# Nine-row loads for two batches, joint attention tails, k split over two queues, and two x tiles by DMA transpose, in a fused linear-attention and Swish-MLP kernel

## Chip, cores, metric

One core of one Trainium2 chip. The metric is the device time of one execution in microseconds (us), the median of several executions; lower is better.

## The reference, cut to what matters

```python
def _attn_ref(q, k, v):                      # 8 batches, 8 heads, 576 rows, 64 columns, f32
    def phi(x): return np.where(x > 0, x, np.exp(x) - 1.0) + 1.0
    q_p, k_p = phi(q), phi(k)
    kv  = np.einsum('bhsd,bhse->bhde', k_p, v)
    z   = np.sum(k_p, axis=2)
    num = np.einsum('bhsd,bhde->bhse', q_p, kv)
    den = np.einsum('bhsd,bhd->bhs', q_p, z)[..., None] + 1e-06
    return num / den

def _moe_ref(x, w_in, w_out, beta):          # x is 4608 x 512, w_in 512 x 2048, w_out 2048 x 512
    h = x @ w_in
    g = h * (1.0 / (1.0 + np.exp(-beta * h)))
    return g @ w_out
```

The attention's output, heads side by side, is the x of the second part.

## The kernel before

Attention (kv, q transposes, num, normalisation, x transposes) is threaded through the large matmuls: H (x times w_in, then Silu) and Y (times w_out) of one batch after the other. The attention of batch b+1 is done during Y of batch b. TensorE does all the matmuls, so below "H1" means the stretch of H matmuls of batch 1, and "Y1" that of its Y matmuls.

576 rows are four tiles of 128 and a tail of 64. Two layouts are used. In the *row form* (all batches but 0) a tensor lies on 128 partitions, four rows of each of eight heads, and the tail on 64 partitions in a second copy. In the *nine-row form* (batch 0 only) half of the heads lie on partitions 0 to 63 and half on 64 to 127, nine consecutive rows on each partition.

```python
def load_rows(dst, src, b, eng=nc.gpsimd):            # row form
    eng.dma_start(out=dst[:, :, 0:NJ, :]...,          # 128 partitions, rows of 512 B
                  in_=src[b, :, 0:MAIN, :].rearrange("h (p j) d -> p h (j d)", j=NJ))
    eng.dma_start(out=dst[0:TAIL, :, NJ, :],          # 64 partitions, rows of 128 B
                  in_=src[b, :, MAIN:S, :].rearrange("h s d -> s h d"))

def load_nine(dst, src, h0=0, h1=HH, j0=0, j1=N9):    # nine-row form, batch 0
    for g in range(2):
        nc.gpsimd.dma_start(
            out=dst[g * TAIL : (g + 1) * TAIL, h0:h1, j0:j1, :]...,     # 64 partitions
            in_=src[0, g * HH + h0 : g * HH + h1, :, :]...)
# ... (cut)
load_nine(k9, k); load_nine(q9, q, j1=4)
# ... identity, v9 in two parts, the rest of q9
for i in range(4):
    nc.gpsimd.dma_start(out=w_in_sb[i], in_=w_in_v[:, :, i * 512 : (i + 1) * 512])
load_w_out(0); load_w_out(1)          # 2 x 512 KB each, f32, 128 partitions, scaled later
load_k(1); load_q(1)
# ... (cut) after the start of batch 0:
load_w_out(2); load_v(1); load_w_out(3)
```

TensorE's start, with warm-up matmuls before there is data, and Y of batch 0 with the attention of batch 1 in it:

```python
warm(10); beta_trans(); make_beta(); warm(20)
exp0(1, 0, 5); ...                               # phi of k, then of q, then kv, num, x of batch 0
# ... (cut)
relu(1, 1); relu(1, 0); w_out_scale(2); phi(1, 1)
v_copy(1)                                        # VectorE, needs v(1)
phi(1, 0)
y_phase_wide(0, {
    9:  [F(kv_mm, 1), F(kv_evac, 1), F(w_out_scale, 3)],
    10: [F(q_trans, 1, 0, 1, wide=True), F(q_trans, 1, 2, 3, wide=True)],
    11: [F(num_mm, 1, 0), F(num_norm, 1, 0)],
    12: [F(num_mm, 1, 1), F(num_norm, 1, 1), F(x_trans, 1, 0, wide=True)],
    # ... (cut)
})
```

Batches 0 to 2 transpose their x tiles on TensorE, batches 3 to 7 by DMA transposes on SyncE's queue (`by_dma(b)`: b >= 3). Each batch has its own tail step of four matmuls with 64 rows of output.

## Time and profile before

297.17 us median of three runs. Starts and lengths of the stretches, read from the timeline of TensorE (first H or Y matmul of each batch), in us:

| | H0 | Y0 | H1 | Y1 | H2 | Y2 | H3 |
|---|---|---|---|---|---|---|---|
| start | 17.16 | 34.16 | 52.53 | 67.61 | 85.25 | 101.19 | 116.38 |
| length | 17.00 | 18.37 | 15.08 | 17.64 | 15.94 | 15.19 | 14.67 |

The bare matmuls of an H or a Y take 13.8 us (64 of 0.216). What a stretch has above that is attention work or waiting; Y0, H0 and Y1 have the most. The lines for this are in the prediction below. The traces' short names: PE is TensorE and PEld its weight loads, DVE VectorE, ACT ScalarE, POOL GpSimd, SPq SyncE's queue. PSUM is the memory that TensorE writes its results to. A timeline line gives: start, duration, engine, line of the source, operation, output and inputs, shape, number of instructions, and in brackets the idle time before it and what ended that.

### The profile page before, as it was taken

To read this page: it belongs to the slowest core of one execution; us is meant where nothing else is said; L and a number is where in the kernel's file an instruction comes from. 1 tells how busy PE (TensorE), PEld (TensorE's weight loads), DVE (VectorE), ACT (ScalarE), POOL (GpSimd) and SP (SyncE) were. 2 spreads that over 40 slices of the span, in tenths; PEclk is the share of its full clock that TensorE was granted. 3 is DMA by queue.
4 is the path that set the end of the run, shared out by engine and by line. 5 is a ranking of instruction groups with operands and counts; after the bars stand their busy time and mean duration, and the time that the engine had idled before them with its cause. 6 is when DMAs were issued, how large, how long until landed. Compare 5 with 4: busy or idle time off the path is not lost.

```text
span 295.1 us, 4750 instructions
## 1 busy us (share of the span) xinstructions
PE 283.9 (96%) x1891; PEld 143.9 (49%) x1912; DVE 124.0 (42%) x261; ACT 175.1 (59%) x234; POOL 52.7 (18%) x72
## 2 busy tenths in 40 slices
PE   8879999999999999999999999999999999999994
PEld 3557445644465544445444544454445444444444
DVE  4765488504365174616461646154715400110012
ACT  2788786889988780778087907790770077018500
POOL 8924474540003200330023000000000000000000
PEclk9999999999999999999999999999999999999999
DMA  7999999999637993699369945024502400120032
GB/s 103 196 207 343 256 272 192 256 193 192 89 142 100 175 131 113 130 174 154 98 129 159 159 109 124 2 71 116 127 0 72 118 36 0 38 90 16 0 73 71
DMA packets 72310, 37.09 MB, mean 126 GB/s; under 512 B 40912, under 2 KB 66784, under 8 KB 72288
## 3 DMA queue, kind: packets, MB, share of 16 engines
q0 software_dynamic: 38912, 20.45, 47.9%
q1 hardware_dynamic: 33216, 16.20, 22.9%
q8 instruction: 15, 0.25, 0.3%
q10 hardware_dynamic: 160, 0.13, 0.2%
q14 instruction: 7, 0.06, 0.1%
HBM read 36.71 MB, written 9.44 MB: 156 GB/s over the span
## 4 chain that ended last, share of the span: by engine, by line
PE 76%; DMA 9%; POOL 4%; ACT 4%; issue 4%; DVE 1%; ACTq 0%; POOLq 0%; DVEq 0%
PE mm L453 37%; PE mm L505 33%; DMA xT<-in_moe_w_out_dram 5%; DMA vraw<-in_v_dram 4%; PE att L399 3%; ACT e L229 2%; POOL xqk L131 1%; PE att L344 1%; PE mm L537 1%; POOL w_in L159 1%; ACT L229 1%; POOL vraw L131 1%; ACT g L445 1%; DVE qk_p L242 0%; POOL xqk L111 0%
## 5 line engine op out<-in xcount | busy, mean ns | idle before, releaser
L445 ACT ACTIVATE g<-mm,beta_c 128x512 bf16<-128x512 f32 (+2 forms) x156 | 97.3, 633 | 88.4 <-PE mm L453 88.1
L505 PE MATMUL mm<-w_out,g 128*128 128x512 bf16 x541 | 126.7, 379 | 1.2 <-issue 0.3
L453 PE MATMUL mm<-xT,w_in 128*128 128x512 bf16 (+2 forms) x560 | 108.1, 349 | 1.4 <-DMA w_in<-in_moe_w_in_dram 1.1
L453 PEld LDWEIGHTS <-w_in 128*128 128x128 bf16 x656 | 61.9, 98 | 62.4 <-DMA w_in<-in_moe_w_in_dram 1.2
L505 PEld LDWEIGHTS <-g 128*128 128x128 bf16 x560 | 53.0, 98 | 58.2
L515 DVE COPY y_sb<-mm 128x512 f32<-128x512 f32 x27 | 18.7, 691 | 70.6 <-PE mm L505 69.1
L229 ACT ACTIVATE e<-xqk 128x2560 bf16<-128x2560 bf16 x14 | 31.9, 2329 | 0.1
L415 DVE TENSOR_TENSOR xs<-att,rden 128x512 bf16<-128x512 f32 (+1 forms) x40 | 27.6, 689 | 1.4
L242 DVE TENSOR_TENSOR qk_p<-r,e 128x2560 bf16<-128x2560 bf16 x14 | 20.9, 1490 | 13.1 <-ACT e L229 12.4
L355 DVE CAST kv_bd<-att 64x130 bf16<-64x130 f32 x28 | 8.2, 292 | 32.2 <-PE att L344 31.8
L72 POOL DMA_DIRECT2D vraw<-in_v_dram x7 | 6.4, 909 | 84.2 <-DVE vaug L370 78.5
L413 DVE TENSOR_SCALAR den<-att 128x8 f32<-128x8 f32 (+1 forms) x40 | 6.5, 161 | 32.0 <-PE att L399 31.9
L399 PE MATMUL att<-kv_bd,q_pT 128*128 128x130 bf16 (+1 forms) x160 | 15.8, 221 | 1.1 <-DVE kv_bd L370 0.7
L399 PEld LDWEIGHTS <-q_pT 128*128 128x128 bf16 (+1 forms) x160 | 11.6, 100 | 10.7 <-DVE xs L415 2.4
L453 PE MATMUL mm<-xT_tail,w_in 128*128 128x512 bf16 x63 | 13.9, 379 | 0.1
L237 DVE TENSOR_SCALAR r<-xqk 128x2560 bf16<-128x2560 bf16 x14 | 11.6, 834 | 3.8 <-DMA xqk<-in_q_dram 2.3
L575 PE MATMUL mm<-g 128*128 128x512 bf16 x34 | 9.9, 452 | 1.2 <-DVE g L143 1.2
L229 ACT ACT_TABLE_LOAD x7 | 9.0, 1283 | 0.1
L414 DVE RECIPROCAL rden<-den 128x8 f32<-128x8 f32 (+1 forms) x40 | 8.1, 202 | 1.4
L72 POOL DMA_DIRECT2D xqk<-in_k_dram x7 | 6.9, 984 | 6.3 <-DMA w_in<-in_moe_w_in_dram 2.8
L76 POOL DMA_DIRECT2D xqk<-in_k_dram x7 | 7.4, 1057 | 1.5 <-DMA w_in<-in_moe_w_in_dram 1.3
L256 ACT ACTIVATE e<-xqk 128x1280 bf16<-128x1280 bf16 (+1 forms) x4 | 4.4, 1155 | 5.4 <-DMA xqk<-in_k_dram 5.3
(71 smaller groups left out, 140.0 us busy)
## 6 DMA issues: line engine op xcount, KB each, us to landing
out_dram<-y_sb SPq DMA_DIRECT2D x28, 256.0 KB, 2.3
xqk<-in_k_dram POOLq DMA_DIRECT2D x7, 512.0 KB, 10.7
xqk<-in_q_dram POOLq DMA_DIRECT2D x7, 512.0 KB, 11.3
vraw<-in_v_dram POOLq DMA_DIRECT2D x7, 512.0 KB, 11.3
w_in<-in_moe_w_in_dram POOLq DMA_DIRECT2D x4, 512.0 KB, 11.0
g<-in_moe_w_out_dram POOLq DMA_DIRECT2D x4, 512.0 KB, 10.9
out_dram<-y_sb SPq DMA_DIRECT2D x14, 128.0 KB, 5.2
xqk<-in_moe_w_out_dram POOLq DMA_DIRECT2D x2, 512.0 KB, 14.4
```

Source lines behind the costliest of these rows:

```text
L72: eng.dma_start(out=dst[:, :, 0:NJ, :].rearrange("p h j d -> p h (j d)"), in_=src[b, :, 0:MAIN, :].rearrange("h (p j) d -> p h (j d)", j=NJ),)
L229: nc.scalar.activation(st[b, "e", a][:, h0:h1], xqk[b % NX][:, a, h0:h1], ACTF.Exp)
L237: nc.vector.tensor_scalar(st[b, "r", a][:, h0:h1], xqk[b % NX][:, a, h0:h1], 0.0, 1.0, ALU.max, ALU.add)
L242: nc.vector.tensor_tensor(st[b, "p"][:, a].rearrange("p j (h d) -> p h j d", h=H)[:, h0:h1], st[b, "r", a][:, h0:h1], st[b, "e", a][:, h0: ...
L355: nc.vector.tensor_copy(kv_bd[b % 2][i][gs, :, g, :], st[b, "kvp"][gs, 2 * i : 2 * i + 2, :])
L399: nc.tensor.matmul(nps[:n, p // 2, c0 : c0 + 2 * (D + 1)], st[b, "qT"][:, t, p, :n], kv_bd[b % 2][p // 2][:, p % 2], start=True, stop=True ...
L415: nc.vector.tensor_mul(xs[:n], nv[:, :, :, 0:D], rden[:n, :, :, None].to_broadcast([n, 2, 4, D]))
L445: nc.scalar.activation(g_sb[b % 2][:, ff, c0:c1], hp[:, c0:c1], ACTF.Silu, scale=beta_c[:, ff : ff + 1],)
L453: nc.tensor.matmul(hp[:, c0:c1], w_in_sb[ff // 4][:, kc, (ff % 4) * P : (ff % 4 + 1) * P], x[:, t0:t1, kc, :] if b < B else x[:, kc, c0:c1 ...
L505: nc.tensor.matmul(yp, g_sb[b % 2][:, ff, t * P : (t + 1) * P], w_out_sb[ff // 4][:, ff % 4, :], start=(ff == 0), stop=(ff == FC - 1),)
L515: nc.vector.tensor_copy(y_sb, yp)
L575: nc.tensor.matmul(st["warm"], g_sb[0][:, FC - 1, 0:P], g_sb[0][:, FC - 1, :], start=True, stop=True, skip_group_check=True,)
```

## The change

The intent is to shorten TensorE's work and waits outside the bare matmuls: load batch 1 in the nine-row form as well (fewer, longer rows; tails of two batches become one step), bring in k of batch 0 by two queues, and give batch 2's last two x tiles to the DMA. The core of the diff (helper functions, evictions and moved steps are cut):

```diff
-        load_nine(dst, src, h0=0, h1=HH, j0=0, j1=N9)        # batch 0 only
+        load_nine(dst, src, b, j0=0, j1=N9, eng=nc.gpsimd)   # any batch, any queue
...
+    load_nine(k_last, k, 0, KF, N9, eng=nc.sync)             # 4 of 9 rows of k, f32, SyncE's queue
-    nc.sync.dma_start(out=beta_row, ...)
+    nc.scalar.dma_start(out=beta_row, ...)
-    load_nine(k9, k)
+    load_nine(x9[0][1][:, :, 0:KF], k, 0, 0, KF)             # 5 of 9 rows, GpSimd
...
-    load_k(1)
-    load_q(1)
+    load_nine(x9[1][1], k, 1)
+    load_nine(x9[1][0], q, 1)
...
-    load_v(1)
+    load_nine(v9[1], v, 1)
...
-    make_beta()
-    warm(20)
+    warm(15)
...                                                          # num: tails of batches b-1 and b together
+            for i in range(1 if t < NJ else 2):
+                bb, n, r0 = (b, P, 0) if t < NJ else (b - 1 + i, TAIL, i * TAIL)
+                nc.tensor.matmul(nps[r0 : r0 + n, ...], st[bb, "qT"][:, t, p, :n], kv_bd[bb % 2]..., ...)
...
-        return b >= DMA_T
+        return b > 2 or (b == 2 and t >= 2) or t == NJ       # x by DMA transpose; all joint tails too
...                                                          # store of batch 1: two copies of 64 rows
-            if b == 0:
+            if b < 2:
...                                                          # batch 2
-                [(ff, 0, 2) for ff in range(4)] + [(ff, 2, 4) for ff in range(4)] + ALL[4:]
+                [(ff, 0, 2) for ff in range(8)] + [(ff, 2, 4) for ff in range(8)] + ALL[8:]
-            plan = { 0: [F(x_trans, 2, 2), F(num_mm, 2, 4), ...], 1: [F(x_trans, 2, 3)], 3: [F(x_trans, 2, 4)] }
...                                                          # later tails: every second batch
-            for t in range(NT):
+            for t in range(NT if n % 2 else NJ):
```

## The prediction

> **What bounds the kernel now.** I read the page first (engine shares, chain), then the busy table by stretches of 2 us for the start, then the timeline of the first 110 us, then the SyncE queue's own timeline, because that queue gets new work.
>
> ```profile
> PE 283.9 (96%) x1891; PEld 143.9 (49%) x1912; DVE 124.0 (42%) x261; ACT 175.1 (59%) x234; POOL 52.7 (18%) x72
> PE 76%; DMA 9%; POOL 4%; ACT 4%; issue 4%; DVE 1%; ACTq 0%; POOLq 0%; DVEq 0%
> ```
>
> TensorE sets the end: from about 85 us on it runs matmuls back to back, and one batch takes 29.85 us (first matmul on H of batch 3 at 116.38, of the later ones every 29.9). A matmul with 512 columns costs 0.216 us there (eight take 1.73 in the chain), so H and Y of a batch are 128 x 0.216 = 27.6 us and cannot move. Whatever the change gains lies in the other work on TensorE, in its waits before 88 us, and in the start.
>
> ```profile
> 2.00:4.00 2.00, 2.00 (x6) 0.73 (x5) 1.60 (x10) 0.23 (x2) 2.00 (x5) 1.00 0.70 97
> 4.00:6.00 2.00, 2.00 (x7) 0.56 (x6) 0.14 (x1) 0.00 (x0) 1.85 (x7) 1.00 1.15 185
> 6.00:8.00 2.00, 2.00 (x11) 0.94 (x10) 1.39 (x6) 0.51 (x1) 2.00 (x4) 1.00 1.24 154
> ...
> 14.00:16.00 2.00, 1.59 (x19) 0.70 (x16) 1.74 (x6) 1.98 (x2) 0.61 (x1) 1.00 1.23 208
> ```
>
> The last column is GB/s: 4 in the first 2 us, 97 in the next two, 154 to 185 to 8 us, then about 205 to 20 us. The transfers are full from 8 us on and short before. What it costs is in the timeline:
>
> ```profile
> 7.49 3.16 ACT L256 ACTIVATE e<-xqk 128x1280 bf16<-128x1280 bf16 x3 [5.25 <-DMA xqk<-in_k_dram]
> ...
> 17.16 1.07 PE L453 MATMUL mm<-xT,w_in 128*128 128x128 bf16 x16 [1.10 <-DMA w_in<-in_moe_w_in_dram]
> ...
> 41.91 1.27 DVE L370 COPY vaug<-vraw 128x2560 bf16<-128x2560 bf16 x1 [0.69 <-DMA vraw<-in_v_dram]
> ...
> 48.69 0.40 PE L433 MATMUL att<-identity,xs 128*128 128x128 bf16 x4
> ...
> 83.07 0.38 PE L433 MATMUL att<-identity,xs 128*128 128x128 bf16 x4 [0.61 <-ACT xT L372]
> ...
> 110.84 0.42 PE L399 MATMUL att<-kv_bd,q_pT 128*64 128x130 bf16 x4
> 111.19 4.86 PEld L505 LDWEIGHTS <-g 128*128 128x128 bf16 x24
> ```
>
> H of batch 0 starts at 17.16 because the first quarter of w_in lands then; attention had its x at 16.3. Batch 1's v lands at 41.9, and from there VectorE works without a pause (v copy, phi of q, four evictions, four w_out scalings, first normalisation) to 48.63; the first x transpose of batch 1 waits for that at 48.69. At 83.07 TensorE waits for an ACT eviction behind a table load.
>
> **What the Trainium skill says.** "DMA: Bandwidth & Descriptors", Issuing engines are not separate DMA queues: copies started from different engines run on the same 16 DMA engines, a second issuer saves only issue time. The trace agrees that the rate is common (205 GB/s of cast data from 8 us on), so the second queue can only fill the short stretch before 8 us. The same page, SWDGE vs HWDGE vs iDMA: a casting DMA must come from GpSimd; hence the SyncE part of k lands as f32 in an idle piece of g. "TensorEngine Tiling (Array Packing)", Key Properties: tiles work independently, but changing the mode drains the array. The trace shows both: 40 matmuls of 65 columns in 128*64 mode take 0.82 us with the pipe, 16 ns apart, less than the 27 ns of one 65-column stream (65/512 x 0.216); and four tail matmuls hold TensorE 0.35 us (110.84 to 111.19) where four 128*128 ones hold it 0.23 (102.92 to 103.15). "Perfetto Trace Analysis", DMA Instruction — HWDGE: a DMA's bar on its queue is descriptor work, not the moving of data. The trace agrees: a transpose of x has a bar of 1.19 us and lands 2.5 us after its start.
>
> **The change, part by part.**
>
> Start. k is split: five of nine rows by GpSimd with cast (two times 160 KB instead of 288), four by SyncE in f32. The bytes read are the same; the gain is what flows before GpSimd's descriptors are there. Up to 8 us the table lacks, against 0.2 MB per us, 0.2 MB in 2 to 4, 0.03 in 4 to 6, 0.09 in 6 to 8: 0.32 MB or 1.6 us. I take 1.25 of it. Then k is complete near 6.1 to 6.4 instead of 7.45, and w_in lands near 15.9. The three exps (3.16 us of ACT) and the kv and x chain move the same 1.2 us, so w_in stays the last thing to arrive. Five warm-up matmuls less (1.1 us) keep TensorE free for the earlier phi. The relu on f32 is slower; by the f32 scalings of w_out (0.48 us for 512 elements) 0.9 instead of about 0.58 us, beside ACT's exps. Gain at H0's start: 1.25 us.
>
> H0. Removed: four tail num matmuls (21.42 to 21.77, 0.35) and the tail transpose (23.96 to 24.18, 0.22). Gain 0.57, so Y0 could start near 32.3 instead of 34.16.
>
> Y0. It does not get all of that. Batch 1 comes in the nine-row form (GpSimd: two copies per tensor with 64x4 rows of 1152 B instead of 1024 rows of 512 B and 512 of 128 B), which I credit with 0.2 us per tensor: k, q and v of batch 1 took about 3.0, 3.3 and 3.3 us between landings, near the rate of the nine-row loads of batch 0. v(1) then lands at 41.9 - 1.25 - 0.6 = 40.05. VectorE from there: copy 0.75 to 1.2, phi 1.33 (1.47 x 2304/2560), clearing the tails 0.75 (new here), evictions 1.2, ones 0.2 (new here), scalings 1.68, normalisation 1.06: 7.0 to 7.45, against 6.75 before. First x transpose at 47.3 against 48.69: gain 1.4. TensorE's own work (kv as 36 matmuls of 130 columns in row pairs, 18 x 0.055 = 1.0 us instead of 0.66; q transposes 36 x 0.0145 = 0.52 instead of 0.97) would have been ready near 46.0, so VectorE after v is the bound. The rest of Y0 has its old 3.84 us. Sum at H1's start: 1.4.
>
> H1. No tail transpose (0.22); the joint tail is eight matmuls in two column halves, about what four cost. Sum 1.65.
>
> Y1. x(2,0) and x(2,1) leave by VectorE, and the second transpose sits one step later. From num(2,0) at 79.33 the steps are: y 0.86, num 0.22, wait for xs to 1.63, y 0.86, num, y 0.86, transpose, then num(2,3), which needs num(2,2)'s buffer and waits for VectorE to about 4.3, y 0.86: 5.42 us instead of 5.92 (79.33 to 85.25). The wait of 0.6 for ACT goes, one of 0.3 for VectorE comes. Gain 0.5, sum 2.15.
>
> H2. Removed: three transposes and the tail num, with their switches. H2 took 15.94 us (85.25 to 101.19) against 64 x 0.216 + 0.75 for kv = 14.57; I take 1.15 of the 1.37. Added: a wait. SyncE must first issue the stores of Y1, which are now two of 64 rows each:
>
> ```profile
> L492 SPq DMA_DIRECT2D out_dram<-y_sb x8: 466/563/603, 49.0 to 53.9; - x8
> ...
> 104.51 1.19 SPq L419 DMA_TRANSPOSE xT<-xs  x1
> ```
>
> In old times: the first y leaves ACT at 82.55 (table load), four stores of 0.47 to 0.56 end at 84.4 to 84.8, transpose(2,2) 1.2, two stores, transpose(2,3) starts at 86.6 to 87.2 and lands 2.5 later, at 89.1 to 89.7. H2 starts at 84.75 and eight half groups of 4 x 0.108 last 3.46, to 88.2. So TensorE waits 0.9 to 1.5 unless the queue is quicker than I count; I enter 0.9. Gain 0.25, sum 2.4.
>
> Later tails. Batches 4 and 6 lose their tail num (0.35 each); batches 3, 5 and 7 do two in about the time of one (plus 0.03 each). Gain 0.6, **sum 3.0 us**. The end, from Y of the tail rows, is not touched.
>
> **Rivals.** (a) The start gives nothing, because both queues share the engines and k's first part is held up by the f32 part. For it: the skill's rule. Against it: the measured hole of 97 GB/s. Then 1.25 is lost at H0 and at v(1): 295.4. (b) v(1) is not the bound: the nine-row loads are much quicker, and Y0 runs at TensorE's pace; 1.0 to 1.3 us more, 293.0. For it: the table's DMA share rises to 1.5 to 1.6 with the many-row loads, against about 1.25 with nine-row ones, at equal GB/s. (c) The SyncE queue serialises worse, the wait in H2 is 2 us: 295.3, or it fits exactly and there is none: 293.3. (d) ACT bounds H2: 16 half SiLUs at 0.445 (88.86 to 90.64, four) against 0.432 per half group on TensorE: 0.2 us, absorbed by four PSUM buffers.
>
> **Range and chances.** 297.17 - 3.0 = 294.2. Rivals a and c together give 296.7, b with no wait in H2 gives 292.1. Range 292.2 to 296.4. 2% is 5.9 us, nearly twice my sum, and needs all terms at their best ends; slower by 2% would need a new wait of 9 us, which nothing shows. Faster 0.04, same 0.95, slower 0.01.
>
> **What would show it.** H0's first matmul near 15.9 with w_in as its releaser; GB/s in 2 to 4 us near 200; first x transpose of batch 1 near 47.3, right after VectorE's first normalisation; H1's start near 51.1; no TensorE wait on ACT in Y1; in H2 after eight half groups a wait of about 1 us on the DMA transpose into xT; only 4 joint tails of eight matmuls, each under 0.45 us. It is wrong if H0 starts at 17 as before, if column halves do not overlap (0.5 us per joint tail), or if TensorE waits in H2 by 2 us and more.

## The result, and the profile after

The changed kernel takes **300.17 us** (299.82 to 300.73, four runs); the kernel before took 296.96 (296.59 to 297.41, four runs) on the same chip. The ratio is 1.0109, with a 95% interval of 1.0086 to 1.0132. Ratios here are the mean time of one kernel's runs over the mean of the other's runs of the same rounds, so not quite the ratio of the medians. The kernel became 1.1% slower: still "same" by the 2% rule, but outside the predicted range of 292.2 to 296.4.

The stretches in the two profiled executions, in us:

| | H0 | Y0 | H1 | Y1 | H2 | Y2 |
|---|---|---|---|---|---|---|
| start before | 17.16 | 34.16 | 52.53 | 67.61 | 85.25 | 101.19 |
| start after | 17.04 | 33.45 | 56.74 | 71.61 | 88.85 | 105.50 |
| length before | 17.00 | 18.37 | 15.08 | 17.64 | 15.94 | 15.19 |
| length after | 16.41 | **23.29** | 14.87 | 17.24 | 16.65 | 15.19 |

Everything that is lost is lost in Y0 (+4.92) and H2 (+0.71). The lines of the page of the changed kernel that answer to the first two of the prediction:

```profile
PE 283.2 (95%) x1894; PEld 145.0 (49%) x1915; DVE 120.0 (40%) x252; ACT 172.7 (58%) x231; POOL 49.5 (17%) x72
PE 77%; DMA 14%; POOL 4%; DVE 2%; issue 2%; POOLq 0%; DVEq 0%
```

TensorE and VectorE have less work than before (0.7 and 4.0 us), and ScalarE too. But in the chain of work that ended last the DMA's share rose from 9% to 14%: the path now waits longer for transfers. Next the busy table by stretches, for the start (columns: stretch, length, busy us and instructions of PE, PEld, DVE, ACT, POOL, granted clock, DMA share, GB/s):

```profile
2.00:4.00 2.00, 2.00 (x6) 0.76 (x5) 0.56 (x6) 0.23 (x2) 2.00 (x4) 1.00 0.84 178
4.00:6.00 2.00, 2.00 (x7) 0.60 (x6) 0.00 (x0) 0.00 (x0) 1.85 (x7) 1.00 1.25 223
6.00:8.00 2.00, 2.00 (x11) 0.93 (x10) 0.46 (x2) 0.47 (x1) 2.00 (x4) 1.00 1.42 195
...
14.00:16.00 2.00, 1.74 (x11) 1.29 (x12) 1.84 (x5) 1.98 (x2) 0.38 (x2) 0.58 1.25 210
```

The hole of 97 GB/s looks filled, as predicted (178). Most of this is only the wider type: SyncE's part of k lands uncast, two copies of 256 KB in f32 (0.52 MB), which would be 0.26 MB after a cast. From 2 to 8 us the changed kernel moved 1.19 MB in place of 0.87, so 0.26 of the 0.32 MB more are the type and no gain. And the granted clock, the share of its full clock that TensorE was given, is 0.58 at 14 to 16 us where it was 1.00. The timeline of the changed kernel, the lines that answer to those shown of before:

```profile
7.53 1.27 ACT L268 ACTIVATE e<-xqk 128x1280 bf16<-128x1280 bf16 x1 [5.29 <-DMA xqk<-in_k_dram]
...
17.04 1.05 PE L494 MATMUL mm<-xT,w_in 128*128 128x128 bf16 x16 [0.29 <-DVE xT L408]
...
45.20 0.76 DVE L362 COPY vaug<-vraw 128x2304 bf16<-128x2304 bf16 x1 [0.75 <-DMA vraw<-in_v_dram]
...
46.02 1.82 PE L342 MATMUL att<-vaug,qk_p 64*128 64x130 bf16 x36 [3.03 <-DVE vaug L362]
...
52.95 0.40 PE L474 MATMUL att<-identity,xs 128*128 128x128 bf16 x4
...
57.50 0.42 PE L440 MATMUL att<-kv_bd,q_pT 128*64 128x130 bf16 x8
...
94.25 7.97 PE L494 MATMUL mm<-xT,w_in 128*128 128x256 bf16 x52 [1.74 <-DMA xT<-xs]
```

Four things are to be seen. k is complete at 7.53, no earlier than before (7.49): SyncE's part is there first (the last packet ended at 5.90 us), GpSimd's part last (6.73). H0 starts at 17.04, and its releaser is now VectorE's copy of x, not w_in. v(1) lands at 45.20 in place of 41.91; TensorE stands 3.03 us for it, and everything after it to H1 is shifted. In H2 TensorE waits 1.74 us for a DMA transpose. The joint tail at 57.50 is eight matmuls in 0.42 us, as cheap as hoped.

SyncE's own queue in H2, as the prediction had it in view:

```profile
86.56 2.40 SPq L535 DMA_DIRECT2D out_dram<-y_sb  x4
89.06 1.24 SPq L460 DMA_TRANSPOSE xT<-xs  x1
...
91.66 1.24 SPq L460 DMA_TRANSPOSE xT<-xs  x1
```

Four store copies of 0.6 us each stand before the first transpose; the second starts at 91.66 and its landing releases TensorE at 94.25.

Where v's 3.3 us come from shows in the DMA view for 28 to 44 us, in which batch 1's k, q and v and the second half of w_out are loaded; the first line is the kernel before, the second the changed one:

```profile
DMA packets 5722, 4.19 MB, mean 262 GB/s; under 512 B 1706, under 2 KB 5182, under 8 KB 5721
```

```profile
DMA packets 2183, 3.77 MB, mean 235 GB/s; under 512 B 155, under 2 KB 1687, under 8 KB 2181
```

The changed kernel needs 2183 packets in place of 5722, and moves 0.42 MB less in the same 16 us. Longer rows did not make the loads quicker.

### The profile page after: what moved, and what is told of

Read it like the earlier page. It is cut to its first block, busy times and chain, and to the rows that moved or that the text cites. A ratio compares the mean times of both kernels' runs of the same rounds, so it can differ in the third digit from the quotient of the medians.

```text
span 298.6 us, 4761 instructions
## 1 busy us (share of the span) xinstructions
PE 283.2 (95%) x1894; PEld 145.0 (49%) x1915; DVE 120.0 (40%) x252; ACT 172.7 (58%) x231; POOL 49.5 (17%) x72
## 4 chain that ended last, share of the span: by engine, by line
PE 77%; DMA 14%; POOL 4%; DVE 2%; issue 2%; POOLq 0%; DVEq 0%
PE mm L494 35%; PE mm L548 34%; DMA xT<-in_moe_w_out_dram 6%; DMA vraw<-in_v_dram 4%; DMA q_pT<-qk_p 3%; PE att L440 3%; POOL xqk L135 1%; PE att L382 1%; PE mm L580 1%; PE att L494 1%; POOL w_in L160 1%; DMA xT<-xs 1%; POOL vraw L135 1%; DVE xs L456 1%; PE att L342 1%
## 5 line engine op out<-in xcount | busy, mean ns | idle before, releaser
L494 PEld LDWEIGHTS <-w_in 128*128 128x128 bf16 x672 | 64.0, 98 | 61.7 <-issue 2.6
L231 ACT ACTIVATE e<-xqk 128x2560 bf16<-128x2560 bf16 x12 | 27.4, 2329 | 0.1
L456 DVE TENSOR_TENSOR xs<-att,rden 128x512 bf16<-128x512 f32 x36 | 24.9, 691 | 1.2
L244 DVE TENSOR_TENSOR qk_p<-r,e 128x2560 bf16<-128x2560 bf16 x12 | 17.9, 1492 | 12.8 <-ACT e L231 12.1
L454 DVE TENSOR_SCALAR den<-att 128x8 f32<-128x8 f32 x36 | 5.9, 163 | 28.1 <-PE att L440 27.8
L440 PEld LDWEIGHTS <-q_pT 128*128 128x128 bf16 (+1 forms) x160 | 10.9, 102 | 10.0 <-DVE xs L456 1.9
L268 ACT ACTIVATE e<-xqk 128x1280 bf16<-128x1280 bf16 (+2 forms) x5 | 7.7, 1562 | 5.3 <-DMA xqk<-in_k_dram 5.3
L410 ACT ACTIVATE q_pT<-att 128x512 bf16<-128x512 bf16 (+2 forms) x8 | 4.9, 649 | 9.7 <-PE att L295 9.7
L239 DVE TENSOR_SCALAR r<-xqk 128x2560 bf16<-128x2560 bf16 x12 | 9.7, 819 | 0.0
L455 DVE RECIPROCAL rden<-den 128x8 f32<-128x8 f32 x36 | 7.3, 203 | 1.2
L494 PE MATMUL att<-xT,w_in 128*128 128x512 bf16 x32 | 7.2, 379 | 0.0
## 6 DMA issues: line engine op xcount, KB each, us to landing
xqk<-in_q_dram POOLq DMA_DIRECT2D x6, 512.0 KB, 12.1
w_in<-in_moe_w_in_dram POOLq DMA_DIRECT2D x4, 512.0 KB, 10.6
```

Source lines behind the costliest of these rows:

```text
L231: nc.scalar.activation(st[b, "e", a][:, h0:h1], xqk[b % NX][:, a, h0:h1], ACTF.Exp)
L239: nc.vector.tensor_scalar(st[b, "r", a][:, h0:h1], xqk[b % NX][:, a, h0:h1], 0.0, 1.0, ALU.max, ALU.add)
L244: nc.vector.tensor_tensor(st[b, "p"][:, a].rearrange("p j (h d) -> p h j d", h=H)[:, h0:h1], st[b, "r", a][:, h0:h1], st[b, "e", a][:, h0: ...
L268: nc.scalar.activation(st[b, "e", a][:, j0:j1].rearrange("p j h d -> p h j d"), in9(b, a, j0, j1), ACTF.Exp,)
L440: nc.tensor.matmul(nps[r0 : r0 + n, p // 2, c0 : c0 + 2 * (D + 1)], st[bb, "qT"][:, t, p, :n], kv_bd[bb % 2][p // 2][:, p % 2], start=True ...
L455: nc.vector.reciprocal(rden[:n], den[:n])
```

## The experiments

The expectations call a stretch in which TensorE is granted half its clock a cold window. All kernels come from one source with a switch for each part; with all switches on its instruction order on each engine is that of the changed kernel, with all off that of the kernel before. Short names: START (k by two queues, 15 warm-up matmuls in place of 20, beta later), NINE1 (batch 1 in nine-row form), JOINT (joint tails, by DMA transpose), XD (batch 2's x tiles by DMA and VectorE, H2 in eight half groups). All gave correct results. The ratio is to the kernel before, run on the same chip.

### Each part by itself

**rows1**: the changed kernel without NINE1.

```diff
-    load_nine(x9[1][1], k, 1);  load_nine(x9[1][0], q, 1)
+    load_k(1);  load_q(1)
...
-    load_nine(v9[1], v, 1)
+    load_v(1)
...                          # and batch 1's exp, phi, kv, q transposes, stores back in row form
```

> The changed kernel with batch 1 alone put back to the old row form (loads and processing). Theory A (the nine-row loads of batch 1 bring v(1) late: 45.2 us against 41.9): v(1) lands by 41 us, the wait of 3.0 us on its copy and the second cold window go, Y0 falls from 23.3 to about 18.5 us, total 295 to 296. Rival B (the second queue at the start disturbs the order of the transfers): v(1) stays at 44 to 45, total about 299 to 300.

Measured: 298.23 us, ratio 1.0038 (0.9994 to 1.0082). v(1) is back at 42.13 and Y0 at 18.83 us, so the loss in Y0 belongs to the nine-row form. But v(1) was expected by 41 us and a total of 295 to 296, and the total fell by only 2 us: a new loss of 4.8 us appears in Y1 (22.47 us in place of 17.64). The waits of TensorE in this run name it:

```profile
PE att L462 <- DMA q_pT<-qk_p: 3.4, 1, 3.4
```

TensorE waits 3.4 us in one go for the DMA transpose of batch 2's q, which landed 12.1 us after its issue (9.0 in the kernel before), and then runs 6.83 us at half clock. The four executions took 296.67 to 299.2 us at mean clocks of 0.994 to 0.981, and the profiled one is of the longer kind, so 4.8 us is the upper end. It is taken up below.

**start_only**: the kernel before with START alone.

```diff
+    load_nine(k_last, k, 0, KF, N9, eng=nc.sync)
-    load_nine(k9, k)
+    load_nine(x9[0][1][:, :, 0:KF], k, 0, 0, KF)
-    make_beta(); warm(20)
+    warm(15)                 # make_beta() after phi
```

> The kernel before with the start of the changed one (k by two queues, beta by ScalarE's queue, late beta, five warm-up matmuls fewer), all else old. Theory A: v(1) lands 1 us earlier than before, at about 40.7; total 296 to 297, less than before only by what H0 gains, because a cold window at 12.5 to 16 us eats the earlier w_in. Rival B: v(1) late (44 to 45), total 300.

Measured: 296.39 us, ratio 0.9993 (0.9974 to 1.0011). H0 starts at 17.12, the clock is at half for 3.41 us from 12.9 us on, and v(1) lands at 42.10, not at the 40.7 expected. The start part gives nothing, the prediction's rival a.

**nine1_only**: the kernel before with NINE1 alone.

```diff
-    load_k(1);  load_q(1)
+    load_nine(x9[1][1], k, 1);  load_nine(x9[1][0], q, 1)
...
-    load_v(1)
+    load_nine(v9[1], v, 1)
```

> The kernel before with batch 1 alone in the nine-row form. Theory A: the loss is whole here: v(1) lands at 45 to 46, TensorE waits 3 us or more in Y0, total 300.5 to 302. Rival B: total within 0.5 us of before.

Measured: 299.97 us, ratio 1.012 (1.009 to 1.015). One part of the change, alone, costs as much as the whole change. v(1) lands at 43.32, TensorE waits 2.0 us for it, and Y0 takes 21.52 us: the right place, but each of the three less than expected (45 to 46, 3 us or more, a total of 300.5 to 302).

**warm20**: the changed kernel with the old number of warm-up matmuls.

```diff
-    warm(15)
+    warm(20)
```

> The changed kernel with 20 warm-up matmuls in place of 15. If the cold window at 12.5 to 16 us comes from the missing warm-up: the clock stays whole there, H0 starts at 16.2 to 16.4 in place of 17.04; but Y0 still waits for v(1), so the total stays within 0.5 us of 300.2. If the cold window has another cause it stays.

Measured: 299.23 us, ratio 1.0098 (1.0063 to 1.0132). The clock stays at full speed, and H0 starts where the prediction had set it:

```profile
16.18 1.05 PE L516 MATMUL mm<-xT,w_in 128*128 128x128 bf16 x16 [0.29 <-DVE xT L430]
```

So the late H0 of the changed kernel is the half clock of a thin warm-up: all six profiled runs with 15 warm-up matmuls had such a window of 3.41 us before 17 us, and of the thirteen with 20 only one (joint_only, at 17.4 us). But H0 0.9 us earlier moved the ratio by only 0.0011, some 0.3 us and within the intervals; v(1) still landed late, at 43.56, and TensorE waited 3.0 us for it.

### Why the nine-row loads are slower

The nine-row form differs from the row form in three ways: rows of 1152 B, two copies per tensor, and 64 partitions per copy. Two kernels keep the row form and its processing, and split the main copy of batch 1's k, q and v in two, once by partitions and once by heads.

**part_halves**: the kernel before, each main copy as two of 64 partitions.

```diff
+        for i in range(2):
+            s = slice(i * TAIL, (i + 1) * TAIL)                    # 64 partitions
-            out=dst[:, :, 0:NJ, :]...,  in_=src[b, :, 0:MAIN, :]...
+            out=dst[s, :, 0:NJ, :]...,  in_=src[b, :, 0:MAIN, :]...[s]
```

> The kernel before, with the main load of q, k and v of batch 1 cut into two copies of 64 partitions each (rows still 512 B). If copies to 64 partitions are what slows the loads: v(1) lands at 43 to 45 in place of 41.9, w_out's 2 KB rows beside them take longer, Y0 grows by 1.2 us or more, total 298 to 299. If row size or the later processing was the cause: v(1) at 42, total within 0.5 us of before.

**head_halves**: the same, each main copy as two of four heads on all 128 partitions.

```diff
+        for i in range(2):
+            s = slice(i * HH, (i + 1) * HH)                        # 4 heads
-            out=dst[:, :, 0:NJ, :]...,  in_=src[b, :, 0:MAIN, :]...
+            out=dst[:, s, 0:NJ, :]...,  in_=src[b, s, 0:MAIN, :]...
```

> The kernel before, with the same loads cut into two copies of four heads each on all 128 partitions: same number of copies and same rows as part_halves. If 64 partitions are the cause: v(1) at about 42, total within 0.5 us of before. If the number of copies in flight is the cause: late like part_halves.

Measured: part_halves 300.07 us, ratio 1.0115 (1.0081 to 1.0149); head_halves 296.82 us, ratio 0.9998 (0.9983 to 1.0013). Same row size, same number of copies, same work on all engines: in the row form the partitions alone cost as much as the whole change did. That the same cause acts in the nine-row form rests on the same slow packets, shown below; nine-row copies to 128 partitions were not tried. The DMA view for 28 to 44 us and the timeline's line of v(1) in part_halves:

```profile
DMA packets 5339, 3.88 MB, mean 242 GB/s; under 512 B 1728, under 2 KB 4829, under 8 KB 5338
```

```profile
44.88 0.83 DVE L443 COPY vaug<-vraw 128x2560 bf16<-128x2560 bf16 x1 [0.81 <-DMA vraw<-in_v_dram]
```

And the same two in head_halves:

```profile
DMA packets 5832, 4.21 MB, mean 263 GB/s; under 512 B 1753, under 2 KB 5296, under 8 KB 5831
```

```profile
41.86 0.83 DVE L443 COPY vaug<-vraw 128x2560 bf16<-128x2560 bf16 x1 [0.93 <-DMA vraw<-in_v_dram]
```

The records of single packets in the traces say which transfers got slower. Mean ns that a packet took, queue of GpSimd, 28 to 44 us (number of packets in brackets):

```
                 4096 B (w_out)   512 B (main rows)   1152 B (nine-row)
before           171 (539)        60 (3476)           -
head_halves      165 (535)        60 (3543)           -
part_halves      211 (509)        60 (3101)           -
nine1_only       227 (514)        60 (116)            109 (1511)
changed kernel   244 (494)        60 (60)             112 (1472)
```

Before 28 us, ahead of batch 1's loads, w_out's packets took 166 or 167 ns in every one of these kernels. So it is w_out's packets, beside copies to 64 partitions, that take longer (in stretches of 2 us up to 378 ns in the changed kernel), while the 512 B rows of those copies still take 60 ns. The delay of v(1) grows in two steps. In the traces GpSimd waits for earlier copies to land before it issues the next: the second half of w_out's third quarter is issued at 32.05 us in part_halves, after a wait of 2.16 for a copy of w_out, and at 30.17 in head_halves, after 0.54, and so the three copies of v are issued 1.2 to 1.5 us later. The rest of the 3.0 us comes between issue and landing. Which of the chip's parts the copies meet at is not in the records, and stays open.

### The second cost, in Y1

**rows1_petail**: rows1 with the joint tail of batches 0 and 1 transposed by TensorE.

```diff
-        return b > 2 or (b == 2 and t >= 2) or t == NJ
+        return b > 2 or (b == 2 and t >= 2) or (t == NJ and b > 1)
...
-            3: [],
+            3: [F(x_trans, 1, 4)],
```

> The run rows1 (changed kernel, batch 1 in row form) with the joint tail of batches 0 and 1 transposed by TensorE in place of a DMA transpose. Theory T (that DMA transpose, issued into a saturated stretch at 54.7 us and landing 8.1 us later, holds up the loads behind it, and so the transpose of q of batch 2): loads keep 190 GB/s at 60 to 64 us, q's transpose lands by 79.5, Y1 falls from 22.5 to 17.3 us, no cold window at 81 to 88, total 294 to 295. Rival (the earlier pace of TensorE or the changed order in Y1 makes the wait): Y1 stays over 20 us and the total near 298.

Measured: 294.1 us, ratio 0.991 (0.9895 to 0.9925), the first version faster than the kernel before. One transpose of 128 x 512 elements less on the DMA is worth 4 us. In rows1, the queue of SyncE, and then the load rate:

```profile
54.72 1.29 SPq L482 DMA_TRANSPOSE xT_tail<-xs  x1
...
69.86 6.91 SPq L448 DMA_TRANSPOSE q_pT<-qk_p  x1
```

```profile
60.00:64.00 4.00, 4.00 (x21) 1.81 (x19) 0.00 (x0) 3.12 (x6) 1.35 (x2) 1.00 1.34 149
```

The same stretch in rows1_petail, and its first num of batch 2:

```profile
60.00:64.00 4.00, 4.00 (x21) 1.82 (x19) 0.00 (x0) 3.12 (x6) 2.52 (x4) 1.00 1.62 189
```

```profile
79.11 0.41 PE L462 MATMUL att<-kv_bd,q_pT 128*128 128x130 bf16 x4 [0.76 <-DMA q_pT<-qk_p]
```

At 54.7 us loads fill the DMA. The transpose issued there landed 8.1 us later (those of H2, with fewer loads beside them, in 2.4), the load rate fell to 149 from 189 GB/s, the loads that follow were issued later (the second copy of q(4) at 62.14 in place of 60.31, v(4) at 64.82 in place of 62.49), and so more of them were still under way when the transpose of q(2) was issued at 69.9: it landed 12.1 us after its issue, against 9.4. TensorE waited 3.4 us, and the half clock followed.

**joint_only**: the kernel before with JOINT alone, to see it without the other parts (edit: JOINT's lines of the diff above).

> The kernel before with the joint tails alone, all of them by DMA transpose. Saved by TensorE: about 0.57 us in H0, 0.2 in H1, 0.6 in H2, 0.46 each in Y3 and Y5: 2.3. Theory T (the DMA transpose of the tails of 0 and 1 in the saturated stretch delays q's transpose): TensorE waits 3 us and more for it in Y1, with a cold window after it, Y1 20 to 22.5 us, total 296.5 to 299. Rival (the wait needed the other parts too): Y1 17.6, total 294.5.

Measured: 298.85 us, ratio 1.0067 (1.0041 to 1.0093). The same wait for q(2) (landing 12.0 us after issue, 3.4 us of waiting, then 3.41 us at half clock), the same load rate (146 GB/s, where the kernel before has 190), Y1 21.28 us. Shown with and without the other parts: the joint tail of batches 0 and 1 by DMA costs more than all joint tails give.

**after_petail**: the changed kernel with that tail transposed by TensorE (same edit as rows1_petail).

> The changed kernel with the tails of 0 and 1 transposed by TensorE. The held-up loads are hidden there behind the 4 us that Y0 loses, so Y1 keeps about its 17 us and the total stays within 0.6 us of 300.2. If the DMA transpose of the tails were a cause of the whole loss: below 298.

Measured: 301.06 us (298.58 to 301.7), ratio 1.0135 (1.0089 to 1.018): 0.9 us above the 300.2 of the changed kernel, where at most 0.6 of difference was expected; a miss, though the interval holds both. In the changed kernel this cost is hidden: v(1) has made TensorE 4 us late, and the transpose of q(2) has landed but for 0.4 us when it is asked for. In this run H2's wait was 2.3 us, with a window of half clock after it.

### The x tiles of batch 2

**xdma_only**: the kernel before with XD alone.

```diff
-            13: [..., F(x_trans, 2, 1, wide=True)],
-            14: [F(num_mm, 2, 3), F(num_norm, 2, 3)],
+            14: [F(x_trans, 2, 1, wide=True, dve=True), F(num_mm, 2, 3), F(num_norm, 2, 3)],
...                          # x(2,2) and x(2,3) by DMA, H2 in eight half groups
```

> The kernel before with batch 2's last two x tiles by DMA transpose and eight half groups alone. Batch 1's stores are single copies here, so both transposes land before the eight half groups end: no wait in H2; Y1 0.1 to 0.8 us shorter, H2 0.6 shorter, total 295.6 to 296.2. If the transposes are late all the same: a wait over 0.5 us in H2 and a total of 297.

Measured: 295.7 us, ratio 0.9969 (0.9954 to 0.9984). H2 takes 15.53 us and waits for no DMA. So the wait of 1.74 us in the changed kernel is not the DMA transposes as such. In rows1_petail, too, where batch 1 is stored by single copies, they start early enough, and H2 takes 14.75 us:

```profile
83.43 1.19 SPq L482 DMA_TRANSPOSE xT<-xs  x1
...
85.34 1.22 SPq L482 DMA_TRANSPOSE xT<-xs  x1
```

**after_actstore**: the changed kernel with the second store of each pair of batch 1 on ScalarE's queue.

```diff
-                    nc.sync.dma_start(
+                    (nc.scalar if b and i else nc.sync).dma_start(
```

> The changed kernel with the second of the two stores of each tile of batch 1 issued on ScalarE's queue in place of SyncE's. If SyncE's four store copies ahead of the two transposes make TensorE wait in H2, that wait falls from 1.74 us to below 0.5 and H2 from 16.65 us to about 15.2. The total stays near 299 (298 to 300), as Y0's 23 us of length are untouched. Rival, the transposes wait for the sums of the tiles or for other transfers: the wait stays above 1.2 us.

Measured: 299.75 us, ratio 1.0111 (1.0074 to 1.0147). No wait for the DMA is left in H2, so SyncE's doubled stores are its cause. But H2 is 16.17 us long, not 15.2, and this is why:

```profile
89.69 0.60 PE L516 MATMUL mm<-xT,w_in 128*128 128x256 bf16 x4 [0.25 <-ACT y_sb L580]
90.72 1.91 PE L516 MATMUL mm<-xT,w_in 128*128 128x256 bf16 x16 [0.43 <-ACT g L508]
92.89 7.97 PE L516 MATMUL mm<-xT,w_in 128*128 128x256 bf16 x52 [0.27 <-ACT g L508]
```

ScalarE, which now issues stores (0.47 to 0.55 us each) between its copies of y, comes late with the Silus, and TensorE waits for PSUM buffers. The wait was exchanged for another; that half of the expectation was wrong.

### The best version, and what the start is worth

**best1**: rows1_petail with 20 warm-up matmuls.

```diff
-    warm(15)
+    warm(20)
```

> As rows1_petail, with 20 warm-up matmuls in place of 15. Clock whole through the start, H0 at 16.2 in place of 17.0; Y0 then waits for v(1) at 42.1 as before, so little of the 0.9 us stays: total 0 to 0.5 us under rows1_petail, and about 1% under the kernel before.

Measured: 293.95 us, ratio 0.9901 (0.9885 to 0.9918). H0 starts at 16.57, but TensorE then waits 1.7 us for v(1) at 42.20. Little is gained over rows1_petail.

**best_nostart**: best1 without START.

> As best1, with the old start (k by one queue, beta by SyncE). If the start part gives nothing because Y0 waits for v(1) anyway: total within 0.4 us of best1 (293.95), v(1) again at about 42. If it gives what was predicted (1.25 us): 295.2.

Measured: 294.33 us, ratio 0.9926 (0.9909 to 0.9943). It ran on another chip than best1, so the pair was run again, five rounds, on one chip.

**best1_5** and **best_nostart_5**: the same two kernels.

> The change with batch 1 back in row form, the first two tails transposed by TensorE, and 20 warm-up operations, compared with the same kernel with the old start (its pair in this call). Theory that v(1)'s landing at 41.8 to 42.2 us bounds Y0 whatever the start does: the two are within 0.3 us of each other, both at a ratio of 0.990 to 0.993 against before. Rival, that the earlier start carries through: this one is 0.8 us or more below its pair (ratio lower by 0.003 or more).

> The same kernel with the old start (H0 at 16.9 to 17.1 us). Theory that v(1) bounds Y0: within 0.3 us of its pair. Rival, the start carries through: 0.8 us or more above it.

Measured: 293.95 us, 0.9917 (0.9904 to 0.993), and 294.48 us, 0.9937 (0.9923 to 0.9951). They are 0.53 us apart, between the two expectations (at most 0.3, at least 0.8), and the intervals overlap: inconclusive. In the traces the lead of 0.48 us at H0 has become 0.31 at H1 and is gone at H2 (84.87 and 84.83). So START's gain is not resolved: the medians say half a microsecond, the traces at H2 nothing.

**v_early**: best1 with v(1) issued ahead of the second half of w_out's third quarter, whose scaling goes to ScalarE. It moves v(1)'s landing on purpose.

```diff
-    load_w_out(2)
-    load_v(1)
+    load_w_out(2, 0, 1)
+    load_v(1)
+    load_w_out(2, 1, 2)
...
+        w_out_scale(2, False, 2, 4)      # ScalarE
-        w_out_scale(2)
+        w_out_scale(2, True, 0, 2)
```

> The best version (row form, first two tails by TensorE, 20 warm-ups), with batch 1's v issued one w_out copy (512 KB, 1.3 to 1.9 us of loading) earlier and the overtaken piece of w_out scaled on ScalarE. Theory that v(1)'s landing sets H1's start (landing plus 10.2 to 10.6 us in row form): v(1) lands near 40.4 instead of 41.75, H1 starts 1.0 to 1.4 us earlier (near 50.8 instead of 51.94), and the kernel takes about 293.1 us, ratio 0.986 to 0.990 against before. Rival, TensorE or the last pieces of w_out set Y0's end as well: H1 starts within 0.4 us of its old place, ratio 0.991 to 0.993.

**best1_again**: best1 unchanged, on the same chip.

> The best version unchanged, on the chip of the run with v earlier: ratio 0.990 to 0.993 against before.

Measured: v_early 295.34 us, ratio 0.9959 (0.9928 to 0.999); best1_again 293.91 us, ratio 0.991 (0.9892 to 0.9927). A miss: slower by 1.4 us, not quicker by 0.8. The timeline of v_early:

```profile
41.14 0.93 DVE L430 COPY vaug<-vraw 128x2560 bf16<-128x2560 bf16 x1 [0.83 <-DMA vraw<-in_v_dram]
...
80.20 0.41 PE L462 MATMUL att<-kv_bd,q_pT 128*128 128x130 bf16 x4 [2.28 <-DMA q_pT<-qk_p]
```

And of best1_again:

```profile
41.66 0.83 DVE L430 COPY vaug<-vraw 128x2560 bf16<-128x2560 bf16 x1 [0.38 <-DMA vraw<-in_v_dram]
...
79.04 0.41 PE L462 MATMUL att<-kv_bd,q_pT 128*128 128x130 bf16 x4 [0.81 <-DMA q_pT<-qk_p]
```

v(1) came only 0.52 us earlier, as k and q of batch 1 came 0.7 and 0.6 later in this run, and H1 started 0.30 earlier (51.56 for 51.86): the direction that the rule gives, too small a step to prove it. What was gained was given back at the next DMA: the transpose of q(2) took 10.9 us to land in place of 9.5.

### What the traces have in common

v(1)'s landing (start of VectorE's copy) and H1's start, one profiled execution each, in us:

| kernel | form of batch 1 | v(1) | H1 | difference | ratio |
|---|---|---|---|---|---|
| before | rows | 41.91 | 52.53 | 10.62 | 1 |
| start_only | rows | 42.10 | 52.29 | 10.19 | 0.9993 |
| head_halves | rows, by heads | 41.86 | 52.05 | 10.19 | 0.9998 |
| best1_again | rows | 41.66 | 51.86 | 10.20 | 0.991 |
| v_early | rows | 41.14 | 51.56 | 10.42 | 0.9959 |
| part_halves | rows, by partitions | 44.88 | 55.06 | 10.18 | 1.0115 |
| nine1_only | nine rows | 43.32 | 54.86 | 11.54 | 1.012 |
| warm20 | nine rows | 43.56 | 55.10 | 11.54 | 1.0098 |
| changed kernel | nine rows | 45.20 | 56.74 | 11.54 | 1.0109 |

H1's start follows v(1) at a fixed distance in each form: in row form 10.2 to 10.6, in nine-row form 11.54. So about 1 us of the nine-row form's loss is not v(1)'s landing but the longer work after it. In row form v(1) lands between 41.1 and 42.2 whatever the start does. In nine-row form it lands 1.4 to 3.3 us later than before; why it varies by 1.9 us among the three was not found out.

## Why the prediction was wrong, step by step

**The reading of the bound was right.** TensorE sets the end, and in Y0 v(1)'s landing and VectorE's chain after it decide. The table above shows it in nine traces.

**The step that failed is Y0, the term "which I credit with 0.2 us per tensor".** It put v(1) at 40.05. It landed at 45.20, 5.15 us later than entered, and that is the larger part of the miss at H1's start (56.74 for 51.1, 5.64 us). The rest, 0.5 us, is the chain after v, entered at 11.05 and measured at 11.54. The credit was for fewer and longer rows and came from batch 0's rate. The runs showed a debit: copies to 64 partitions slow the copies of w_out beside them, and v(1), queued behind them all, comes 3 us later (part_halves against head_halves). The prediction looked at row sizes and did not ask how many partitions a copy writes. One of the pages that it cites had the warning: the Trainium skill, "DMA: Bandwidth & Descriptors", Rules for kernel authors, says of two transfers to disjoint partition halves not to bother, as they serialise, and to use one transfer of 128 partitions. No run here tests whether they serialise; what this case shows is the price of not heeding it, 1.15% in part_halves. Rival b, quicker loads, had the wrong sign; no rival had slower loads.

**Start: −1.25 entered, −0.12 measured at H0 and nothing at v(1).** Two terms failed. The first is the sum of missing transfers: it counted 0.32 MB of room up to 8 us, at a rate measured on cast data, and forgot that SyncE's part lands as f32, twice the bytes. That part's 0.26 MB of excess fills most of the room; an estimate from these numbers leaves 0.06 MB, 0.3 us at the prediction's 0.2 MB per us. So k was complete at 7.53, not at 6.1 to 6.4. The second: five warm-up matmuls less, which were to keep TensorE free, let the clock fall: 0.57 and 0.58 of full speed at 12 to 16 us. With 20, H0 starts at 16.18. But with the old start and 20, H0's start lies anywhere from 16.20 (nine1_only) to 17.26 (joint_only) in eight traces, so what START gives at H0 cannot be read from single traces. The Trainium skill, "TensorE: Matmul & The Clock Gate", Why this matters for your kernels, says that idle gaps of TensorE above some 3 us bring half speed back. The traces agree only in part. The wait of 3.4 us in rows1 is followed by half clock, and in the changed kernel a second window, at 46.5 to 49.9 us, follows the wait of 3.03. But the first one, from 12.3 us on, follows no wait longer than 0.73 us; a wait of 2.0 us has a window after it in nine1_only and in after_petail, and the waits of 2.9 to 3.1 us in part_halves, warm20 and after_actstore have none. Rival a was right in its result: start_only is at 0.9993.

**H0: −0.57 entered, −0.59 measured.** Right.

**H1: −0.25 entered, −0.21 measured.** Right, and column halves overlap: eight joint tail matmuls took 0.42 us, and Y2, Y4 and Y6, with two tails each, are as long as before (15.19).

**Y1: −0.5 entered, −0.40 measured, but right only by a disguise.** The part hides a cost that the prediction did not see, the transpose of the first joint tail amid the loads. It lengthens Y1 by 4.8 and 3.6 us in rows1 and joint_only; in the changed kernel the 4 us lost in Y0 give q(2) the time to land.

**H2: −0.25 entered, +0.71 measured.** The mechanism was right (SyncE's stores ahead of the transposes) and the size off: the wait was 1.74 us where 0.9 was entered and 0.9 to 1.5 held possible. The stores came at 86.56 to 88.96, as four of 0.6 us, not of 0.47 to 0.56. Two other runs with both parts waited 2.1 and 2.3 (warm20, after_petail), the prediction's rival c.

**Later tails: −0.6 entered, −0.9 measured.** Y3 and Y5 are each 0.46 shorter.

The sum: −0.12 − 0.59 + 4.92 − 0.21 − 0.40 + 0.71 − 0.90 = +3.4 us, and the spans of the two profiled executions differ by 3.5. The parts of the change that shorten TensorE's work are worth what was said: without the nine-row form and with the first joint tail on TensorE, the rest gives 294.1 us, near the 294.2 predicted for the whole, but by another route, so that this is luck. A slip in the prediction's sums: by its own terms rivals a and c together give 296.55, not 296.7, and both this and its low figure of 292.1 lie outside the range that it gave.

**What stays open.** Where in the chip the 64-partition copies and w_out's copies meet; why v(1)'s landing varies by 1.9 us among nine-row runs; whether START gives half a microsecond or none; which length or pattern of TensorE's waiting brings a window of half clock.

## What to carry to other kernels

Where a load is on the path, ask how many partitions each copy writes before counting its rows: two copies of 64 partitions cost 3 us here against two of 128 with the same rows and bytes. A DMA transpose issued where loads fill the DMA delayed those loads here (149 for 189 GB/s) and the next transpose behind them (12.1 for 9.4 us); look at the load rate there before moving work off TensorE. Count a transfer in the type in which it lands: bytes that are only wider look like a filled gap. And when a change in one stage is undone, look at the next wait: two costs of some 4 us each lay behind each other here, and only one could be seen at a time.

## What the Trainium skill lacked or had wrong

- "DMA: Bandwidth & Descriptors", Rules for kernel authors, says of transfers to partition halves that they serialise, and "SBUF — State Buffer", which the prediction did not look at, has lower rates for a transfer to 64 partitions than to 128. Neither says that such copies slow other copies beside them: packets of 4096 B to 128 partitions took 211 to 244 ns beside 64-partition copies, 165 to 171 without, and the data moved in 16 us fell from 4.21 to 3.88 MB.
- "DMA: Bandwidth & Descriptors", same section, says that a transpose next to ordinary DMAs needs nothing, which is about correctness. It does not give the price: a transpose of 128 x 512 elements in a stretch full of loads landed after 8.1 us (2.4 elsewhere), the load rate fell from 189 to 149 GB/s, and the next large transpose landed after 12 us in rows1 and joint_only (9.0 to 9.8 in most runs without it, and 9.1 in the changed kernel, where it was issued 4 us later).
- The same page, Issuing engines are not separate DMA queues, held: a second queue raised a stretch from 97 GB/s to 178, mostly by the wider type, and the tensor split over both queues was complete no earlier (7.53 us and 7.49).
- "TensorE: Matmul & The Clock Gate", Part 1: The HAM clock gate, gives the window as 3413 ns, and the windows here measure 3.41 us. Its limit of some 3 us of idle time did not decide here: windows came after waits of no more than 0.73 and of 2.0 us, and none after three waits of 2.9 to 3.1. It gives no measure of how dense a warm-up must be up to the first real work: 15 matmuls where 20 stood brought such a window before 17 us in six profiled runs of six.
